# A seven-product scheme for the second channel product of an attention and MLP-mixer kernel

## The chip, the cores and the metric

One core of one Trainium2 chip runs the whole kernel in one launch. The core has five engines that run side by side and meet only at semaphores: TensorE (in the profile PE for its matmuls and PEld for its weight loads), VectorE (DVE), ScalarE (ACT), GpSimd (POOL) and SyncE (SP). The metric is the device time of one execution in microseconds (us); lower is better. Before the change it was 307.08 us, the median of three runs (306.64 to 309.66).

## The reference, cut to what matters

The input is attention over 4 batches, 8 heads, 768 tokens and 64 features per head, with a block mask, followed by a mixer MLP on 512 channels:

```python
scores = scale * np.matmul(q, k.transpose(0, 1, 3, 2))
...
attn_out = np.matmul(attn, v)                     # (4, 8, 768, 64)
x = attn_out.transpose(0, 2, 1, 3).reshape(4, 768, 512)
tok = np.einsum('ts,bsd->btd', w_tok, alpha1 * x + beta1)
u = x + lam * tok
a2 = alpha2 * u + beta2
ch = np.maximum(a2 @ w_ch1, 0.0) @ w_ch2          # 512 -> 2048 -> 512
return u + lam * ch
```

The last product, relu(...) @ w_ch2, is the "second channel product". Per batch it is a 768 x 2048 matrix times a 2048 x 512 matrix. The change concerns this product alone, and what makes room for it.

## The kernel before, in words

All steps of the program are short functions, registered under a letter by `@on`, and the text `ORDER` (L47 to L118) names them one after the other in the order in which they are emitted. `pin_order` (L121) keeps every engine in exactly that order, so the place of a word in the table is the place of its instructions in its engine's queue. `bank_order` (L138) keeps the eight PSUM banks apart: who writes a bank waits for all who read it last, whatever part of the bank they read. The table was written out by a planner and holds the bank numbers (`q8:1`) and the engine of some steps (`g14:a` for ScalarE, `g15:d` for VectorE).

The work of one batch, step by step:

- `q` (L575) makes 1024 scores per partition in two PSUM banks, `e` (L599) takes their exponential on ScalarE into an `eT` tile (eleven buffers, `NET`), `m` (L606) masks that tile in place on VectorE by a minimum with a 0 or 65504 mask (for head pairs 5 to 15; earlier pairs have the mask in the product), and `p` and `r` (L638, L642) multiply it with the values. `nt` and `n` (L646, L659) divide by the row sums and put the result into `x_sb`, which has room for three batches.
- `a`, `b`, `k`, `x` (L697 to L728) are the token mixing; `x` adds the product into `x_sb` in place, so that `x_sb` then holds u. `u` casts u to bf16 and `U` transposes it, by DMA on SP's queue or on TensorE, into `uT` (three buffers).
- `f` (L779) is the first channel product: for a half batch of 384 tokens and one of 16 blocks of hidden features, four matmuls of 384 columns. `g` (L791) adds the bias, takes the relu and writes bf16 into `hts`, on ScalarE or VectorE. `hts` has two buffers, each a half batch: [128 features, 16 blocks, 384 tokens].
- `h` (L813) is the second channel product. For each half batch `kk` and each of three groups of 128 tokens, 16 matmuls of 512 columns run through the 16 blocks (four steps `h` of four matmuls); the lam factor was put into the weights `w2b` beforehand by `S`. The last group is cut in two halves of 256 columns.
- `o` (L825) adds the finished bank to `x_sb` on VectorE, into a separate tile `ot`, and `s` (L835) sends that tile to HBM from SP's queue.

So `hts` of one half batch can be refilled while `h` works on the other half. Most of the table mixes the attention of a later head pair (`q e m p`) with the mixing of an earlier batch; from the end of the attention on, only `f`, `g`, `h`, `o` and `s` are left.

Of the kernel before, what the change touches and what calls it, by code (L numbers as in the profile page):

```python
# [36 lines left out]
TH = 256  # L37
NU = 9
NPE = 5
NET = 11  # L40
# [7 lines left out]
lv0 lk1 lq1 cq0 hm0 lt1 q0:2 q1:0 e0 q3:3 H1:2 q2:2 e1 hq1:d hk1:d lq2 e2 z480:3 z480:3 z480:3 q4:0  # L48
q6:1 q5:2 lk2 lv1 e3 cv0:d lq3 cq1:d e4 lt0 ck1:d p0:6 p1 p2 p3 e5 r4:7 q7:0 p4 e6 e7 lt2 lk3 n0
H2:5 H3:4 r5 hk2:d hq2:d lc2 lc0 q8:1 e8 r6 W2:6 hq3:d w2:d F21 cq2:d lc1 ck2:d q9:0 W3:5 q12:1 r7  # L50
e9 r8 e12 q11:0 n1 hk3:d H4:6 e11 cv1:d cq3:d q10:1 lk4 lv2 H5:7 q16:0 e10 p9:4 hq4:d q15:1 hk5:d
p10 e16 e15 p11 lq6 lq4 q13:0 hk4:d e13 hq5:d w3:d p12 W1:7 w1:d q14:1 W0:5 w0:d q25:0 p13 q19:3 e14
W4:5 r13:3 W5:2 n2 e25 ck3:d w4:d e19 lv4 lk5 lx3 q22:0 H6:4 e22 w5:d r14 q20:3 r15 H7:2 q17:0 hq6:d
r16 hk6:d q18:2 e20 L1 e17 L0 a0 e18 q24:3 q23:0 r17 b0 e24 hq7:d F22 cv2:d n3 k1:4 q26:3 k0:5 x1
cq4:d lv3 lc5 lk6 hk7:d e23 q21:0 p18:4 q28:1 e26 lx1 e21 e28 x0 q29:3 r22:5 p19 r23 q31:0 r24 r25
cq6:d r26 a1 F23 ck4:d lv6 ck5:d u1:d u0:d lw0 lq7 lw3 lc4 lw1 e29 b1 cv4:d n5 q30:1 p20 p21 H9:7
e31 p22 H8:6 q27:0 e30 n4 hq9:d cv3:d hk9:d U0:5 lw2 e27 q34:1 k3:4 hk8:a v0:d e34 lx2 p27:7 q33:0
lq5 x3 e33 hq8:d F24 p28 q32:2 a2 k2:6 q35:1 e32 p29 b2 u3:d q37:0 ck6:d F25 x2 q44:2 u2:d p30 r31:6
p31 e35 lk7 e44 r32 r33 U1:3 lx0 lv7 q39:2 r34 lq8 n6 F26 ah6 r35 k5:7 n7 M0 v1:a q40:1 ah7 e39 x5
e37 bh7 e40 bh6 F27 k4:6 q38:2 e38 L2 cv6:d q36:0 k7:2 B0 x4 F28 e36 cq7:a u4:d x7 u5:d q41:2 k6:6  # L60
lk8 lv8 x6 e41 p36:7 u7:a q43:0 U2:2 q42:2 u6:d v2:a U3:6 e43 p37 S6 v3:d p38 p39 p40 f15:6 f12:3
f10:2 e42 f14:0 g14:a g15:d f13:5 f29:6 f7:4 f8:1 S7 g12:d S4 g13:a g7:a S2 g10:d n8 S5 ck7:a g29:d
f6:2 f30:3 f23:5 f11:7 f28:6 cq5:d lv5 f9:0 g23:d g6:a g8:d f22:2 g11:d g9:d g30:d g28:a lq9 g22:d
f31:4 f0:5 f2:1 f25:7 f4:0 S0 g31:a f3:6 tq5 g2:d g3:d S1 g4:a g0:a N0 tk5 tk6 f27:2 f24:3 f5:0
f21:6 f26:1 f16:5 F29 g5:d g21:d O0 g24:d g26:d F30 S3 r40:4 g27:a g25:a cv5:a r41 tq7 g16:a r42 r43
r44 q47:0 n9 q51:3 q48:1 f17:5 lk9 e47 a4 f20:4 e51 e48 f1:0 f18:1 f19:2 g1:a b4 g20:d F31 k9:4
g17:a g19:a g18:d F32 q52:0 q53:3 q50:1 tq6 cq8:a k8:5 lv9 cv7:d m51 m48 x9 P7:d e52 p48:1 p51:4 m52
lq10 e53 cq9:a e50 x8 m53 p52 h0:0 F33 ck9:d p53 h1 lk10 lv10 nt17 ck8:d q49:3 q45:1 q46:2 tk8 tk7
h2 lq11 tq8 e49 F34 m50 e45 m49 h3 p49 p50 q59:1 q56:3 e46 o0 m47 m46 e59 u8:d tq9 tk9 e56 m59 u9:d
m45 m56 nt16 q58:2 h8:0 h9 P0:a e58 h4:2 h5 h10 F35 P4:d m58 h11 cq11:d P6:d o2 p45:3 lk11 p46 s0  # L70
ck10:a p47 cv8:d nt15 F36 h6 lv11 a5 q57:2 q62:3 q61:0 b5 e57 h7 e61 k11:4 e62 m57 lq12 p57:5 q60:0
o1 ck11:d P1:d x11 m62 q55:1 F37 e60 s1 q70:3 p58 p59 lk12 nt19 m61 F38 m60 h20:4 cq12:d e55 h21 m55
# [118 lines left out]
def kernel(  # L191
# [99 lines left out]
    b1_bc = wk.tile([P, DM], FP, name="b1_bc", tag="ot", bufs=4)  # L291
    a2T = pp.tile([P, 4], FP, name="a2T", tag="a2T")
    b1_bcb = pp.tile([P, DM], BF, name="b1_bcb", tag="b1_bcb")
    warm = pp.tile([P, 512], BF, name="warm", tag="warm")
    nc.vector.memset(warm[:], 0.0)

    def zero(w, i):
# [587 lines left out]
```

## Time and profile before

| what | value |
|---|---|
| median of three runs | 307.08 us (306.64 to 309.66) |
| the profiled execution, first to last instruction (its span) | 306.8 us; the page gives no other time of its own |
| mean granted TensorE clock | 1.000 |
| busy: TensorE matmuls / VectorE / ScalarE / GpSimd | 298.7 / 219.0 / 198.5 / 51.4 us |
| first matmul of the first `q` | 7.6 us into the span |
| last matmul ends, last `o` ends, span ends | 303.3, 303.8, 306.8 us |

Busy time counts an instant once when several instructions of an engine overlap; a row's mean duration counts each of them in full. The two differ on VectorE, ScalarE and TensorE, where the next instruction starts before the last one has ended, so an engine's cost per instruction is read from how far apart the starts lie in a stretch without waits, and its latency from the mean. A line such as `L820 PE MATMUL` belongs to a line of the kernel; the letters of the steps do not appear in the profile and are found by these lines.

### The profile page before, as it was taken

The page shows a single profiled execution, that of the slowest core. Times are in us where ns is not written, and L with a number is a line of the kernel's source. Part 1 is how long each engine was busy: PE and PEld are TensorE (multiplying, and loading weights), DVE is VectorE, ACT ScalarE, POOL GpSimd, SP SyncE. Part 2 cuts the span into 40 slices and gives each one's busy share as a digit, 9 for nine tenths or more (in the row PEclk, how much of TensorE's full clock was granted, in tenths as well). Part 3 has the DMA queues.
Part 4 walks back from the last instruction along what each step waited for, and adds up shares of the span by engine and source line. Part 5 has one row for each costly group of instructions (what it writes and reads, how often), then busy time and mean ns, then how long its engine had stood idle before and what let it go on. Part 6 is the DMA issues. An engine that isn't in the chain of part 4 may idle for free.

```text
span 306.8 us, 7748 instructions
## 1 busy us (share of the span) xinstructions
PE 298.7 (97%) x3276; PEld 195.2 (64%) x3301; DVE 219.0 (71%) x476; ACT 198.5 (65%) x262; POOL 51.4 (17%) x94
## 2 busy tenths in 40 slices
PE   8999999999999999999999999999999999999995
PEld 4577788766756676557666675556666585565443
DVE  3479999897979998865878697568778897412112
ACT  3799999745985996876954885276974961256000
POOL 5553655121334402310010000000000000000000
PEclk9999999999999999999999999999999999999999
DMA  6999999999999889941012345420002303100112
GB/s 144 177 238 186 133 195 198 203 193 178 118 146 178 133 158 150 153 63 30 2 28 60 87 88 88 112 60 2 2 2 61 96 2 84 39 2 0 67 68 106
DMA packets 48319, 30.92 MB, mean 101 GB/s; under 512 B 29004, under 2 KB 44124, under 8 KB 48284
## 3 DMA queue, kind: packets, MB, share of 16 engines
q0 software_dynamic: 15936, 15.21, 32.6%
q1 hardware_dynamic: 32132, 14.97, 22.9%
q8 instruction: 26, 0.43, 0.6%
q10 hardware_dynamic: 216, 0.24, 0.2%
q14 instruction: 9, 0.07, 0.1%
HBM read 31.19 MB, written 6.88 MB: 124 GB/s over the span
## 4 chain that ended last, share of the span: by engine, by line
PE 84%; DVE 10%; issue 2%; ACT 2%; DMA 1%; SPq 0%; DVEq 0%; ACTq 0%
PE psum L786 27%; PE psum L820 22%; PE psum L719 10%; PE psum L617 9%; PE psum L593 7%; PE psum L583 6%; DVE eT L611 3%; ACT eT L604 2%; DVE a1p L689 2%; DVE x_sb L652 1%; DMA sampi<-in_sampled_blocks_dram 1%; DVE a1p L695 1%; DVE ot L830 1%; PE psum L335 1%; PE psum L298 1%
## 5 line engine op out<-in xcount | busy, mean ns | idle before, releaser
L604 ACT ACTIVATE eT<-psum 128x1024 f16<-128x1024 f32 (+1 forms) x145 | 138.3, 1023 | 36.4 <-PE psum L593 31.8
L820 PE MATMUL psum<-w2b,hts 128*128 128x512 bf16 (+1 forms) x375 | 85.2, 370 | 2.1 <-issue 0.8
L786 PE MATMUL psum<-uT,w1b 128*128 128x384 bf16 (+1 forms) x512 | 85.4, 326 | 0.0
L611 DVE TENSOR_TENSOR eT<-eT,maskT 128x1024 f16<-128x1024 f16 x99 | 65.4, 686 | 8.3 <-ACT eT L604 8.0
L786 PEld LDWEIGHTS <-w1b 128*128 128x128 bf16 x512 | 49.2, 98 | 33.9 <-issue 1.1
L820 PEld LDWEIGHTS <-hts 128*128 128x128 bf16 x400 | 36.5, 98 | 37.6 <-issue 2.3
L800 ACT ACTIVATE hts<-psum,b1t 128x384 bf16<-128x384 f32 x73 | 38.8, 586 | 32.2 <-PE psum L786 31.6
L802 DVE TENSOR_SCALAR hts<-psum,b1t 128x384 bf16<-128x384 f32 x55 | 33.0, 615 | 28.3 <-PE psum L786 27.6
L617 PEld LDWEIGHTS <-eT 128*128 128x128 f16 x1152 | 42.6, 97 | 8.6 <-issue 1.3
L617 PE MATMUL psum<-vext,eT 128*128 128x65 f16 x1152 | 45.9, 193 | 0.0
L719 PE MATMUL psum<-a1p,wtokT 128*128 128x128 bf16 x576 | 36.0, 219 | 1.1 <-DVE a1p L695 1.0
L719 PEld LDWEIGHTS <-wtokT 128*128 128x128 bf16 x576 | 33.2, 98 | 5.3 <-issue 2.7
L830 DVE TENSOR_TENSOR ot<-x_sb,psum 128x512 f32<-128x512 f32 (+1 forms) x25 | 16.6, 663 | 20.1 <-PE psum L820 20.1
L583 PE MATMUL psum<-qx,kx 88*128 88x512 bf16 (+1 forms) x120 | 27.7, 348 | 0.2
L593 PE MATMUL psum<-qx,kx 64*128 64x256 bf16 x396 | 27.7, 271 | 0.0
L593 PEld LDWEIGHTS <-kx 64*128 64x128 bf16 x396 | 16.5, 94 | 10.1 <-issue 3.7
L728 DVE TENSOR_TENSOR x_sb<-x_sb,psum 128x384 f32<-128x384 f32 x32 | 17.4, 549 | 4.8 <-PE psum L719 4.6
L401 POOL DMA_DIRECT2D k<-in_k_dram x15 | 10.8, 717 | 35.8 <-ACT vext L383 17.4
L401 POOL DMA_DIRECT2D v<-in_v_dram x16 | 11.6, 724 | 25.1 <-ACT b1t L383 7.0
L689 DVE TENSOR_TENSOR a1p<-x_sb,a_bc 128x768 bf16<-128x768 f32 (+1 forms) x17 | 15.4, 908 | 0.3
L652 DVE TENSOR_TENSOR x_sb<-psum,rcp 128x256 f32<-128x256 f32 x33 | 14.0, 424 | 1.1
L583 PEld LDWEIGHTS <-kx 88*128 88x128 bf16 x120 | 10.2, 103 | 6.1 <-issue 1.8
(70 smaller groups left out, 160.8 us busy)
## 6 DMA issues: line engine op xcount, KB each, us to landing
out_dram<-ot SPq DMA_DIRECT2D x23, 256.0 KB, 2.1
v<-in_v_dram POOLq DMA_DIRECT2D x16, 192.0 KB, 4.7
k<-in_k_dram POOLq DMA_DIRECT2D x15, 192.0 KB, 5.0
q<-in_q_dram POOLq DMA_DIRECT2D x15, 192.0 KB, 6.2
w2b<-in_moe_w_ch_dram POOLq DMA_DIRECT2D x4, 512.0 KB, 11.1
w1b<-in_moe_w_ch_dram POOLq DMA_DIRECT2D x4, 512.0 KB, 12.0
wtk<-in_moe_w_tok_dram POOLq DMA_DIRECT2D x3, 384.0 KB, 7.5
mask_rows<-maskT SPq DMA_DIRECT2D x1, 576.0 KB
```

What stands on the lines that cost most here:

```text
L401: nc.gpsimd.dma_start(t[:], pair_ap(src, *batch(p)))
L583: nc.tensor.matmul(t[:, f : f + w], kx[h][0:KC, ts(jt, P)], qx[h][0:KC, c : c + w], start=True, stop=True,)
L593: nc.tensor.matmul(t[:, (2 * a + j) * TH : (2 * a + j + 1) * TH], kx[h][r, ts(2 * g + j, P)], qx[h][r, ts(th, TH)], start=True, stop=True,)
L604: nc.scalar.activation(eTs[n][:, c], t[:, c], AF.Exp, bias=EXPB, scale=SCALE)
L611: nc.vector.tensor_tensor(out=e, in0=e, in1=mask, op=ALU.min)
L617: nc.tensor.matmul(ops[key][:, t * VW : t * VW + D + 1], eTs[n][:, c : c + P], vext[n // NU % NV][:, a, jt, 0 : D + 1], start=(first and z ...
L689: nc.vector.tensor_tensor(out=a1p[p][:, :, c : c + w], in0=x_of(p, 0, NT, c, w), in1=per_col(a1_bc, p, NT, c, w), op=ALU.mult)
L719: nc.tensor.matmul(t[:, j, :], wtokT[:, s, ts(3 * g + j, P)], a1p[p][:, s, :], start=(s == 0), stop=(s == NT - 1),)
L786: nc.tensor.matmul(hps[i][:, 0:w], w1b[:, dk, ts(f, P)], uT[b][:, dk, hf * HS : hf * HS + w], start=(dk == 0), stop=(dk == 3),)
L800: nc.scalar.activation(hts[kk][:, f, :], t[:, 0:HS], AF.Relu, bias=b1t[:, f : f + 1], scale=1.0)
L802: nc.vector.tensor_scalar(out=hts[kk][:, f, :], in0=t[:, 0:HS], scalar1=b1t[:, f : f + 1], scalar2=0.0, op0=ALU.add, op1=ALU.max,)
L820: nc.tensor.matmul(cps[i][:, 0:w], hts[kk][:, nk, ts(m, P)], w2s[0][:, nk, lo : lo + w], start=(nk == 0), stop=(nk == 15),)
```

## The change

The half batches y = 0 and y = 1, the two halves h = 0 and 1 of the hidden blocks, and the two halves of the weights' rows and columns are taken as 2 x 2 block matrices, once for each of the three token groups q of 128 (named q in the code, not to be mixed up with the step `q`). Write A11, A12 (y = 0), A21, A22 (y = 1) for the quadrants of `hts`, each [128, 8 blocks, 128 tokens], and B11 to B22 for those of `w2b`, each [128, 8 blocks, 256 columns]. The seven products z of Winograd's form of Strassen's scheme, eight matmuls of 256 columns each, are

- z0 = A11 B11, z1 = S1 T1, z2 = S2 T2, z3 = S3 T3, z4 = A22 T4, z5 = S4 B22, z6 = A12 B21, with S1 = A21 + A22, S3 = A11 - A21, S2 = S1 - A11, S4 = A12 - S2 and T1 = B12 - B11, T2 = B22 - T1, T3 = B22 - B12, T4 = B21 - T2.

One PSUM bank serves a batch and a token group: z0, z2, z3 and z4 accumulate in its left half one after the other, and after each of them the half is read out; z1 and z5 accumulate in its right half; z6 begins the left half anew. The new steps are

- `T` (four in all): the sums of weight quadrants, VectorE, 2048 elements per partition each.
- `A` (four for each of 12 batch and token groups, 48 in all): the sums S1 to S4, VectorE, 1024 elements each; S3 and S2 are written over A21 and A11 in place, S1 and S4 go to tiles `ss` with three buffers.
- `h`: 84 steps of eight matmuls of 256 columns, in place of 100 steps of four.
- `o`: five additions per group straight into `x_sb`, three of 256 columns and two of 512, and one more at the very end (61), in place of 25 into `ot`.
- `s` sends rows of `x_sb` itself; 25 transfers as before.

Beside these, `m` leaves out four columns at each edge of every 128 tokens (`EDGE`), whose queries lie in the first and the last block and see everything: 960 elements instead of 1024. `eT` has ten buffers instead of eleven, `uT` two instead of three, `ot` and `warm` no longer have room of their own. The order table is new from end to end; in it, 88 of the 128 `g` (73 before) and 22 of the 32 `u` (16) are on ScalarE, and 12 of the casts of loaded heads (13).

```diff
-NET = 11
+NET = 10
...
-    lam_bc = wk.tile([P, DM], FP, name="lam_bc", tag="ot", bufs=4)
-    b1_bc = wk.tile([P, DM], FP, name="b1_bc", tag="ot", bufs=4)
+    lb = wk.tile([P, 2, DM], FP, name="lb", tag="tt", bufs=3)
+    lam_bc, b1_bc = lb[:, 0, :], lb[:, 1, :]
...
-        e = eTs[n][:].rearrange("p (a c) -> p a c", a=4)
+        c = slice(EDGE, P - EDGE)
+        e = eTs[n][:].rearrange("p (a t c) -> p a t c", a=4, t=2)[:, :, :, c]
         th, g = divmod(n % NU, 3)
-        mask = maskT[:, g, ts(th, TH)].unsqueeze(1).broadcast_to([P, 4, TH])
+        mask = maskT[:, g, ts(th, TH)].rearrange("p (t c) -> p t c", t=2)[:, :, c]
+        mask = mask.unsqueeze(1).broadcast_to([P, 4, 2, P - 2 * EDGE])
         nc.vector.tensor_tensor(out=e, in0=e, in1=mask, op=ALU.min)
...
-            uT[b] = wk.tile([P, 4, S + 16], BF, name="uT", tag="uT", bufs=3)
+            uT[b] = wk.tile([P, 4, S + 16], BF, name="uT", tag="uT", bufs=2)
...
+    HF = FF // P // 2
+    HD = DM // 2
+    def quadrant(b, q, y, h):
+        return hts[2 * b + y][:, h * HF : (h + 1) * HF, ts(q, P)]
+    def weights(h, c):
+        return w2s[0][:, h * HF : (h + 1) * HF, c * HD : (c + 1) * HD]
+    def quad(n, k):
+        b, r = divmod(n, 3 * k)
+        return (b,) + divmod(r, k)
+    def total(op, out, in0, in1):
+        nc.vector.tensor_tensor(out=out, in0=in0, in1=in1, op=op)
...
+    @on("T")
+    def _(j):
+        if j != 1:
+            w2t[j] = wk.tile([P, HF, HD], BF, name="w2t", tag="tt", bufs=3)
+        if j == 0:
+            total(ALU.subtract, w2t[0][:], weights(1, 1), weights(0, 1))
+        elif j == 1:
+            total(ALU.subtract, weights(0, 1), weights(0, 1), weights(0, 0))
+        elif j == 2:
+            total(ALU.subtract, w2t[2][:], weights(1, 1), weights(0, 1))
+        else:
+            total(ALU.subtract, w2t[3][:], weights(1, 0), w2t[2][:])
+    def new_sum(key):
+        sums[key] = wk.tile([P, HF, P], BF, name="ss", tag="ss", bufs=3)
+        return sums[key][:]
...
+    @on("A")
+    def _(n):
+        b, q, j = quad(n, 4)
+        a11, a12, a21, a22 = (quadrant(b, q, y, h) for y in range(2) for h in range(2))
+        if j == 0:
+            total(ALU.add, new_sum((b, q, 1)), a21, a22)
+        elif j == 1:
+            total(ALU.subtract, a21, a11, a21)
+        elif j == 2:
+            total(ALU.subtract, a11, sums[b, q, 1][:], a11)
+        else:
+            total(ALU.subtract, new_sum((b, q, 4)), a12, a11)
...
     @on("h")
-    def _(i, bank_=None):
-        i, r = divmod(i, 4)
-        kk, m, lo, w = part(i)
-        if r == 0:
-            cps[i] = bank(bank_, [P, DM])
-        for nk in range(4 * r, 4 * r + 4):
+    def _(n, bank_=None):
+        b, q, z = quad(n, 7)
+        if z == 0:
+            cps[b, q] = bank(bank_, [P, DM])
+        lhs = sums[b, q, 1 if z == 1 else 4][:] if z in (1, 5) else quadrant(b, q, z in (3, 4), z in (4, 6))
+        rhs = (weights(0, 0), weights(0, 1), w2t.get(2), w2t.get(0), w2t.get(3), weights(1, 1), weights(1, 0))[z]
+        side = z in (1, 5)
+        for nk in range(HF):
             nc.tensor.matmul(
-                cps[i][:, 0:w], hts[kk][:, nk, ts(m, P)], w2s[0][:, nk, lo : lo + w],
-                start=(nk == 0), stop=(nk == 15),
+                cps[b, q][:, side * HD : (side + 1) * HD], lhs[:, nk, :], rhs[:, nk, :],
+                start=(z in (0, 6) and nk == 0), stop=(nk == HF - 1), skip_group_check=True,
             )
...
     @on("o")
-    def _(i):
-        kk, m, lo, w = part(i)
-        b, hf = half(kk)
-        ots[i] = wk.tile([P, DM], FP, name="ot", tag="ot", bufs=4)
-        nc.vector.tensor_tensor(
-            out=ots[i][:, 0:w], in0=x_sb[:, b % NXB * NT + 3 * hf + m, lo : lo + w],
-            in1=cps.pop(i)[:, 0:w], op=ALU.add,
-        )
+    def _(n):
+        b, q, r = quad(n, 6)
+        last = (b, q) == (B - 1, 2)
+        y, lo, hi, c = ((0, 0, 1, 0), (0, 1, 2, 0), (1, 1, 2, 0), (1, 0, 2, 0), (0, 0, 2, 0), (0, 0, 1, 0))[r]
+        if last and r == 4:
+            lo = c = 1
+        sl = x_sb[:, b % NXB * NT + 3 * (1 - y) + q, lo * HD : hi * HD]
+        total(ALU.add, sl, sl, cps[b, q][:, c * HD : (c + hi - lo) * HD])
...
         nc.sync.dma_start(
-            out[b].rearrange("(p o) d -> p o d", o=NT)[:, 3 * hf + m, lo : lo + w], ots.pop(i)[:, 0:w]
+            out[b].rearrange("(p o) d -> p o d", o=NT)[:, o, lo:hi], x_sb[:, b % NXB * NT + o, lo:hi]
         )
```

A number after `h` counts 21 to a batch and seven to a token group, one after `A` 12 and four, one after `o` 18 and six. The first words of the last stretch of the new table, where the attention has ended and the first channel product is ending too, and its last words, are

```
f108:6 h77:0 f111:1 h70:2 f110:3 g104:a A44 A40 A36 o66 A41 h63:7 h78 f109:4 A45 A46
h79 f107:5 g110:a g107:a g108:d o54 A42 o60 o67 g109:d h71 g111:a h80 A47 o68 A37 A38
...
h83 h75 o71 h68 h69 o58 s11 s8 s20 s13 s23 s6 s21 s12 s22 s14 s24 s15 s18 h76 o64 s19
```

## Prediction

> **What bounds the kernel now.** I read the busy shares first, then the stretches of 15 us, then the chain for the pace of each kind of work, then the rows of the groups.
>
> ```profile
> PE 298.7 (97%) x3276; PEld 195.2 (64%) x3301; DVE 219.0 (71%) x476; ACT 198.5 (65%) x262; POOL 51.4 (17%) x94
> ```
>
> TensorE is the bound. Its matmul rows overlap, so 97% says little; the stretches show what stands beside it:
>
> ```profile
> 30.00:45.00 15.00, 14.67 (x234) 11.93 (x232) 14.64 (x36) 14.06 (x16) 9.29 (x15) 1.00 1.04 163
> 90.00:105.00 15.00, 14.83 (x180) 9.19 (x181) 14.43 (x37) 11.62 (x14) 6.20 (x11) 1.00 0.93 153
> 270.00:285.00 15.00, 14.95 (x90) 8.62 (x89) 3.09 (x5) 8.00 (x17) 0.00 (x0) 1.00 0.00 1
> 285.00:300.00 15.00, 14.95 (x74) 7.24 (x74) 3.16 (x5) 0.00 (x0) 0.00 (x0) 1.00 0.19 71
> ```
>
> The columns behind the length are PE, PEld, DVE, ACT, POOL, then clock, DMA share and GB/s. Twice VectorE is already as full as TensorE (14.64 and 14.43 of 15 us), and only behind the attention is it idle. The clock is 1.00 throughout. Paces come from the chain (start, length, what, how many):
>
> ```profile
> 57.02 17.64 PE psum L786 x108
> 177.47 1.29 DVE eT L611 x2
> 179.36 3.01 DVE eT L611 x5
> 187.18 2.17 PE psum L719 x36
> 282.77 0.86 PE psum L820 x4
> ```
>
> An `f` matmul takes 163 ns, a 512-column `h` matmul 216 ns, a 128-column one 60 ns, weight load included. A mask starts every 0.60 us although its row says 0.69. The tail's 256-column matmuls fill this stretch, where weight loads of 98 ns were busy 0.90 us, 9.2 loads, so 109 ns each:
>
> ```profile
> 301.00:302.00 1.00, 1.00 (x12) 0.90 (x10) 1.00 0.66 254
> ```
>
> ```profile
> L820 PE MATMUL psum<-w2b,hts 128*128 128x512 bf16 x343 | 82.1, 379 | 2.1 <-issue 0.8 <-DVE x_sb L652 0.3
> L611 DVE TENSOR_TENSOR eT<-eT,maskT 128x1024 f16<-128x1024 f16 x99 | 65.4, 686 | 8.3 <-ACT eT L604 8.0
> L800 ACT ACTIVATE hts<-psum,b1t 128x384 bf16<-128x384 f32 x73 | 38.8, 586 | 32.2 <-PE psum L786 31.6
> L802 DVE TENSOR_SCALAR hts<-psum,b1t 128x384 bf16<-128x384 f32 x55 | 33.0, 615 | 28.3 <-PE psum L786 27.6
> L830 DVE TENSOR_TENSOR ot<-x_sb,psum 128x512 f32<-128x512 f32 x23 | 15.7, 684 | 18.6 <-PE psum L820 18.6
> L695 DVE TENSOR_TENSOR a1p<-a1p,b_bcb 128x768 bf16<-128x768 bf16 x15 | 8.3, 555 | 0.4
> L477 DVE TENSOR_TENSOR w2b<-w2b,lam_bcb 128x1024 bf16<-128x1024 bf16 x8 | 5.4, 683 | 0.0
> L830 DVE TENSOR_TENSOR ot<-x_sb,psum 128x256 f32<-128x256 f32 x2 | 0.8, 420 | 1.5 <-PE psum L820 1.5
> ```
>
> Two prices per VectorE instruction follow: the mean (latency), and the mean less 0.085 us (0.686 against 0.60) when the next one doesn't depend on it.
>
> How full TensorE really is: every step of the old table at its pace (`f` 0.652, late `q` 0.254, early `q` 0.435, `p` 0.245, `k` 1.065, `h` 0.864 us) comes to 290.8 us. The first `q` starts at 7.6 and the last matmul ends at 303.3, so stalls cost only 4.9 us; 3.5 us follow it. Any gain must come from less matmul work, and stays only if VectorE and ScalarE keep up.
>
> **TensorE's part.** Removed: 92 full `h` steps of 0.864 and 8 half ones of 0.436, 83.0 us. Added: 84 steps of eight matmuls at 109 ns, 0.87 us each, 73.1 us. Saved: 9.9 us, all on the bounding engine. The ends for the pace are 108 ns (half of 216) and 125 ns (32 of them in 4.0 us busy, starts and waits included), with which nothing would be saved; I take 109, from the stretch without gaps. The weight loads, 672 instead of 400, hide: 98 ns fit in 109, and loads follow each other at 60 ns in L719.
>
> **VectorE's part**, at the price between independent starts. Added: 48 `A` of 1024 bf16 elements, the form of L477 (0.683, so 0.60): 28.8 us. Four `T` of 2048: L695 and L477 give 0.5 ns per element, so 1.195, less 0.085, 1.11 each: 4.4 us. `o`: per group three of 0.335 and two of 0.60, 2.2 us, 26.8 in all with the extra one, against 15.0. Taken off: 15 `g` to ScalarE, 8.3 us; 6 `u`, 2.8; 64 elements of each of 99 masks at 0.5 ns, 3.3. Casts: 0.3 more. Sum: 31 us more, 207.0 to 237.9 by this price (219.0 measured before: dependent ones cost more). Ends: `A` as slow as fp32 additions (L830, 1.04 ns per element) would be 25 us more; L477 and L695, with runs as short, speak against it. For the shorter runs of the mask I take the gain; without it 3.3 us return.
>
> **ScalarE's part.** 15 `g` and 6 `u` more, one cast less: 200.7 to 211.7 us.
>
> **The other queues.** GpSimd issues the same loads, the transposes on SP are the same. Freed by `s` being in place: `ot`. New waits: `nt` of batch 3 (`nt36`) needs slots that batch 0's output has left; its last `s` (`s4`) stands about ten TensorE us earlier, and such a transfer lands in 2.1 us: nothing. On SP, `s20` waits for `o70`, some eight `h` (7 us) before the end, with ten transfers of 256 KB queued behind it, five of them ready long ago, and one of 128 KB. 2.9 MB in all at the 377 GB/s that the last 7 us reach when busy (113 at a share of 0.30) are 7.6 us. The last `o` is 0.26 us longer (0.684 for 0.42) and its transfer 0.4 us (2.1 for 1.7). I take 0.7 us; the queue makes 0.7 to 3.
>
> **New waits of TensorE.** A bank is read between z0, z2, z3, z4 and z6: four hops of `o` per group, 3 x 0.42 + 0.68, 1.9 us, 23 us in all were nothing beside them; a gain is excluded, since the old `h` waited in mid-bank for nothing. The table always has another group's `h` (0.87 us each) or attention in between. In the tail 21 `h` and four `f` (20.9 us) face 12 `A` and 16 `o` (about 14 us) with three banks in turn: I take nothing. `hts` has no free buffer now: `g63`, the first into batch 1, must wait for all of batch 0's z3 and z4. The table puts attention there; that is in the next sum. Two buffers of `uT` and ten of `eT` I cost at nothing: `f` of batch 0 is over long before `U8`, and a score and its use stand 12.3 us of TensorE work apart at the median (7.2 before).
>
> **Where VectorE and ScalarE come up short.** I added the prices in the order of both tables; these are us of PE / DVE / ACT in the new one: to `r44` 49.4 / 40.3 / 47.0; to `h6` 61.0 / 60.8 / 63.1; to `h22` 48.6 / 43.6 / 45.5; to `h42` 57.5 / 46.7 / 39.5; to `p143` 12.8 / 13.0 / 4.9; to the end 51.5 / 33.5 / 11.6. In the second stretch all three are full. Cutting both tables in windows of 12, 15, 18, 21 and 24 us of TensorE work (six offsets each) and adding, per window, what the fullest engine has beyond TensorE gives 10.3, 6.1, 5.1, 5.3, 4.7 us now against 2.8, 1.4, 0.5, 0.4, 0.4 before: 7.5, 4.7, 4.6, 4.9, 4.3 more, 5.2 in the mean. I take 5.2, on top of the 4.9 there already. Ends: zero, if buffers carry work across; and the full durations, in the rival below.
>
> **Sum**, against the profiled span: 306.8 - 9.9 + 0.7 + 5.2 = 302.8 us. The median of the runs stands 0.3 above the span: 303.1.
>
> **Rival 1: the cover holds.** No extra stalls: 306.8 - 9.9 + 0.7 + 0.3 = 297.9 us. For it: 30 to 45 us, where PE, DVE and ACT are at 14.67, 14.64 and 14.06 of 15, and to 57.0 us the work (48.3 us) is only 1.1 us late. Against it: that was one stretch, not 61 us with ScalarE 2 us over.
>
> **Rival 2: VectorE becomes the bound (slower).** If sums and additions depend on each other so closely that each costs its full mean, the windows of 12 us, the distance between a score and its use, hold 23.2 us of excess against 8.6: 14.6 more. 306.8 - 9.9 + 0.7 + 14.6 + 0.3 = 312.5 us. Place: between `r44` and `h6`, where full durations give VectorE 69.7 us to TensorE's 61.0, and around `h42`, where seven `A` stand together. It decides from 9.2 us of extra stalls, and is 1% slower from 12.3. For it: 219.0 measured lies 40% of the way from 207.0 to the 237.5 that full means give. Against it: the masks at 0.60 above. The Trainium skill, VectorE: DVE Perf Modes, section "The DRAIN you can't avoid", says that the next instruction doesn't start until the pipe is empty. By that rule this rival would be the forecast; the trace, with starts 0.60 us apart for rows of 0.69, disagrees for independent instructions.
>
> **Rival 3: the gain is eaten.** With VectorE 40% of the way to the full means, the mean extra of the five windows (5.2 and, at full means, 12.0) becomes 7.9: 305.8 us, within 1%. For it, the same 40%; against it, the table can put independent work between dependent ones.
>
> **How the numbers follow.** About 1%, from 304.0 to 310.2 us, is what a measurement of this kernel can tell from no change. Forecast 0.48 (300.5 to 305, two thirds of it below 304.0), rival 1 0.16, rival 3 0.13, rival 2 0.23 (all but 0.01 beyond 310.2). Faster: 0.33 + 0.16 = 0.49; same 0.15 + 0.13 + 0.01 = 0.29; slower 0.22. The range, 298 to 311, leaves out half of rival 1 and about half of rival 2.
>
> **What would show it.** Right: 256-column `h` matmuls 109 ns apart; `A` rows near 0.68 us, masks near 0.65; VectorE busy near 250 us; TensorE waiting longest between about 57 and 125 us, for ScalarE or VectorE. The tail from the first of the last 21 `h` is some 21 us plus 4. Wrong: `A` at 1.2 us; matmuls waiting on `o` in the tail; TensorE waiting on `A` throughout; the last transfer landing over 3 us after its `o`; a granted clock below 1.00 after such waits.

## The result, and the profile after

The changed kernel takes 319.59 us (median of four runs, 318.20 to 320.94) against 306.86 us (306.06 to 309.66) for the kernel before on the same chip: a ratio of 1.041, interval 1.035 to 1.047. It is slower, by some 12.7 us, where 303.1 us were predicted, and it lies outside the range of 298 to 311 us. The profiled execution took 318.20 us with a span of 316.4 us, 9.6 us longer than the span of before. It is the shortest of the four; the other three have spans of 317.6 to 319.1 us and left no profile, so the account below is of 9.6 us and not of 12.7. All ratios in this document leave out executions more than 1.5% above the fastest of their kernel.

The page of the kernel after: busy times, then the TensorE, clock and DMA rows of the 40 slices (7.9 us each).

```profile
PE 292.7 (93%) x3573; PEld 220.1 (70%) x3573; DVE 247.8 (78%) x539; ACT 208.3 (66%) x287; POOL 50.3 (16%) x94
...
PE   7999997039999999999999999999999999999993
...
PEclk9999999558999999999999999999999999999999
DMA  6999999994772153799638134320000104400036
```

TensorE is busy 6 us less and VectorE 29 us more (9.9 and 31 were worked out). The loss is a hole: two slices, from 55 to 71 us, in which TensorE stands almost still, the clock granted to it falls to a half, and the DMA row reads 9. After the hole TensorE is full to the end. The stretches say the same (PE, PEld, DVE, ACT, POOL, then clock, DMA share, GB/s):

```profile
30.00:45.00 15.00, 15.00 (x257) 12.51 (x255) 14.16 (x35) 13.93 (x17) 9.52 (x16) 1.00 1.19 178
...
45.00:60.00 15.00, 8.17 (x130) 6.65 (x127) 8.80 (x28) 8.88 (x10) 4.46 (x10) 0.88 1.24 185
60.00:75.00 15.00, 6.20 (x75) 5.14 (x76) 2.40 (x8) 2.56 (x4) 0.71 (x1) 0.55 1.14 193
75.00:90.00 15.00, 14.88 (x121) 8.11 (x119) 14.55 (x33) 14.22 (x29) 3.20 (x8) 1.00 0.53 67
90.00:105.00 15.00, 15.00 (x216) 10.42 (x213) 14.05 (x31) 14.57 (x22) 2.12 (x4) 1.00 0.44 59
```

The kernel before has TensorE busy 15.00 of 15 us in both of the stretches with the hole:

```profile
45.00:60.00 15.00, 15.00 (x228) 12.03 (x225) 12.99 (x35) 12.81 (x17) 5.19 (x10) 1.00 1.15 201
60.00:75.00 15.00, 15.00 (x107) 9.21 (x106) 12.50 (x30) 7.78 (x18) 2.62 (x6) 1.00 1.21 179
```

In the kernel after, all four engines are idle for most of the time from 60 to 75 us while the DMA queues are at work: they wait for transfers. (The DMA share alone does not tell the two kernels apart: it is above 1 in both.) TensorE's waits (us in total, times, longest) name the one it is, and the chain of waits shows it whole (start, length, what):

```profile
PE psum L596 <- DMA kx<-rel: 15.5, 1, 15.5
```

```profile
53.36 0.71 SPq L555
...
54.16 14.51 DMA kx<-rel
...
68.80 0.61 PE psum L596 x4
```

L596 is the late `q`, L555 the transposing load `tk`. It is the score `q61`, the first of head pair 6 and the first in the new table to need a DMA transpose. SP's queue shows how late that transpose was, after and then before:

```profile
43.83 10.23 SPq L555 DMA_TRANSPOSE qx<-rel  x1
54.16 4.63 SPq L555 DMA_TRANSPOSE kx<-rel  x1
59.89 0.36 SPq L507 DMA_DIRECT2D maskT<-mask_rows  x1
```

```profile
66.34 5.93 SPq L552 DMA_TRANSPOSE kx<-rel  x2
73.48 0.36 SPq L504 DMA_DIRECT2D maskT<-mask_rows  x1
73.95 3.97 SPq L552 DMA_TRANSPOSE qx<-rel  x2
```

To issue one transpose took 10.23 and 4.63 us in the kernel after, 1.3 to 3 in the one before (two stand together in some rows), and the one of `kx` stood behind the one of `qx`. From issue to landing `kx` took 14.5 us against 5.6 to 7.9, in the views of the tile `kx` after and before:

```profile
DMA to landing us min/median/max: 14.5/14.5/14.5
```

```profile
DMA to landing us min/median/max: 5.6/6.7/7.9
```

The new table starts them at 44 and 54 us, into the loads of both channel weights (`w1b` landed 14.3 us and `w2b` 15.6 us after issue at the median; before, 12.0 and 11.1), and wants the first one at 53.4 us; the old table put 27 `f` in front and asked at 74.7 us. VectorE's queue was held by the same traffic: the cast `cq5` waited 9.6 us for its load.

Adding every step of the new table at its pace gives 49.7 us of TensorE work up to the first `f` and 231.2 us from there on. So the span divides into the following; the two rows of stalls are remainders, what is left of a stretch when the work at its pace is taken off.

| us | before | after |
|---|---|---|
| up to the first `q` | 7.6 | 7.1 |
| TensorE work | 290.8 | 280.9 |
| stalls up to the first `f` (57.0 us / 73.45 us) | 1.1 | 16.6 |
| stalls behind it | 3.8 | 6.4 |
| from the last matmul to the end | 3.5 | 5.3 |

By this account the saving of 9.9 us is there (the eighth product below bears it out). The front lost 15.5 us more than before, the rest of the table 2.6, the tail 1.8.

### The profile page after: what moved, and what is told of

It reads as the page before. It is cut to its first block, busy times and chain, and to the rows that moved or that the text cites. A ratio compares the mean times of both kernels' runs of the same rounds, so it can differ in the third digit from the quotient of the medians.

```text
span 316.4 us, 8394 instructions
## 1 busy us (share of the span) xinstructions
PE 292.7 (93%) x3573; PEld 220.1 (70%) x3573; DVE 247.8 (78%) x539; ACT 208.3 (66%) x287; POOL 50.3 (16%) x94
## 4 chain that ended last, share of the span: by engine, by line
PE 83%; ACT 7%; DMA 5%; DVE 2%; issue 1%; SPq 0%
PE psum L792 24%; PE psum L871 23%; PE psum L623 11%; PE psum L725 10%; PE psum L596 8%; ACT eT L607 5%; DMA kx<-rel 5%; PE psum L586 4%; ACT hts L806 2%; PE psum L301 1%; PE psum L338 1%; PE psum L770 1%; PE psum L463 1%; DVE a1p L695 0%; ACT vext L386 0%
## 5 line engine op out<-in xcount | busy, mean ns | idle before, releaser
L806 ACT ACTIVATE hts<-psum,b1t 128x384 bf16<-128x384 f32 x88 | 48.7, 584 | 37.6 <-PE psum L792 27.8
L617 DVE TENSOR_TENSOR eT<-eT,maskT 128x960 f16<-128x960 f16 x99 | 61.9, 651 | 2.2 <-ACT eT L607 1.7
L596 PE MATMUL psum<-qx,kx 64*128 64x256 bf16 x396 | 30.5, 273 | 15.7 <-DMA kx<-rel 15.5
L830 DVE TENSOR_TENSOR x_sb<-x_sb,psum 128x256 f32<-128x256 f32 (+1 forms) x61 | 31.2, 516 | 12.0 <-PE psum L871 11.8
L871 PE MATMUL psum<-w2t,hts 128*128 128x256 bf16 x288 | 35.3, 273 | 0.0
L596 PEld LDWEIGHTS <-kx 64*128 64x128 bf16 x396 | 15.6, 94 | 26.5 <-issue 19.1
L808 DVE TENSOR_SCALAR hts<-psum,b1t 128x384 bf16<-128x384 f32 x40 | 24.2, 614 | 11.8 <-PE psum L792 11.2
L871 PE MATMUL psum<-w2b,hts 128*128 128x256 bf16 x192 | 24.6, 273 | 0.0
L871 PE MATMUL psum<-w2b,ss 128*128 128x256 bf16 x192 | 24.6, 273 | 0.0
L871 PEld LDWEIGHTS <-ss 128*128 128x128 bf16 x192 | 18.2, 98 | 2.5 <-issue 0.4
L386 ACT CAST ub<-x_sb 128x384 bf16<-128x384 f32 x22 | 11.2, 514 | 10.3 <-DVE x_sb L734 10.2
L830 DVE TENSOR_TENSOR ss<-hts 128x1024 bf16<-128x1024 bf16 x24 | 16.2, 683 | 0.9 <-ACT hts L806 0.8
## 6 DMA issues: line engine op xcount, KB each, us to landing
w2b<-in_moe_w_ch_dram POOLq DMA_DIRECT2D x4, 512.0 KB, 15.6
w1b<-in_moe_w_ch_dram POOLq DMA_DIRECT2D x4, 512.0 KB, 14.3
```

The source lines that it names most:

```text
L596: nc.tensor.matmul(t[:, (2 * a + j) * TH : (2 * a + j + 1) * TH], kx[h][r, ts(2 * g + j, P)], qx[h][r, ts(th, TH)], start=True, stop=True,)
L617: nc.vector.tensor_tensor(out=e, in0=e, in1=mask, op=ALU.min)
L806: nc.scalar.activation(hts[kk][:, f, :], t[:, 0:HS], AF.Relu, bias=b1t[:, f : f + 1], scale=1.0)
L808: nc.vector.tensor_scalar(out=hts[kk][:, f, :], in0=t[:, 0:HS], scalar1=b1t[:, f : f + 1], scalar2=0.0, op0=ALU.add, op1=ALU.max,)
L830: nc.vector.tensor_tensor(out=out, in0=in0, in1=in1, op=op)
L871: nc.tensor.matmul(cps[b, q][:, side * HD : (side + 1) * HD], lhs[:, nk, :], rhs[:, nk, :], start=(z in (0, 6) and nk == 0), stop=(nk == H ...
```

## The experiments

The theory: TensorE takes its queue in order, and the front of the new table asks for DMA transposes some 20 us earlier than the old one, in the middle of a backlog on the DMA engines. The rivals: VectorE's sums are the bound (the prediction's rival 2), the clock makes the loss, or the transposes are slow by themselves. Times are medians; the ratio is to the kernel before, measured beside each run (306.7 to 308.1 us).

**The sums on VectorE.** All `A` and `T` return at once and the products take plain quadrants and weights.

```diff
     @on("A")
     def _(n):
+        return
...
     def _(j):
+        return
```

> Edit: the kernel after without its operand sums: the 48 steps A and the 4 steps T are left out, the products take plain quadrants and plain weights in their place (so the second channel product is wrong), the seven products and the additions o stay. Some 33 us of VectorE work are gone. Backlog theory: the wait at the first transposed score stays at 14 to 16 us and the time at 316 to 320 us, within 1% of the kernel after. VectorE-bound rival: the time falls by 8 us or more, to below 311 us.

318.23 us, ratio 1.039 (1.029 to 1.049); span 316.9. VectorE was busy 216.4 us instead of 247.8, and the time stayed within the spread of the two kernels' runs (317.29 to 321.55, and 318.20 to 320.94):

```profile
PE psum L596 <- DMA kx<-rel: 15.2, 1, 15.2
```

31 us of VectorE work are worth nothing that these runs can show: rival 2 is refuted as the cause. Nor did the part behind the hole get shorter: from the first `f` to the end it is 243.6 us here and 243.2 in the kernel after.

**An eighth product.** The third product of every group is done twice (the output is wrong by it).

```diff
-        for nk in range(HF):
+        for nk in [*range(HF), *range(HF if z == 2 else 0)]:
```

> Edit: the kernel after with an eighth product in every group (the third one is done twice, so the result is wrong): 12 x 8 matmuls of 256 columns more, 10.5 us of TensorE at the measured 109 ns. If TensorE bounds the part behind 75 us, as its windows say (15.00 of 15 us busy), the time rises by 8 to 11 us, to 327 to 331 us: the saving of the seven-product scheme was real and was only outweighed. If VectorE bounds it, the time rises by less than 4 us.

329.12 us, ratio 1.072 (1.067 to 1.078), 9.5 us above the kernel after by the medians, 11.5 by the spans (327.9). One product in every group costs about what its 96 matmuls at 109 ns make, 10.5 us. So the product left out was worth that much, and the loss lies elsewhere.

**The mask's traffic away.** The late pairs' mask (a table of 576 KB sent to HBM by `N0` and brought back by `O0`) is left out; a fill takes its place, so pairs 5 to 15 are not masked.

```diff
-        nc.sync.dma_start(maskT[:], mask_dr.rearrange("(p g) w -> p g w", p=P))
+        nc.gpsimd.memset(maskT[:], F16MAX)
-... lk8 lv8 N0 tq6 tk6 O0 e40 ...
+... lk8 lv8 tq6 tk6 O0 e40 ...
```

> The changed kernel without the mask's way through HBM: the write of 576 KB is left out and the read of 576 KB is replaced by a memset on GpSimd (so the late pairs are not masked). Theory (bandwidth of the DMA engines): 1.15 MB less at some 200 GB/s is 5 to 6 us less, the wait of 15.5 us at q61 falls to 8 to 11 and the time to 312 to 315 us. Rival (the order on SP's queue or the cast cq5 alone sets it): the wait stays over 13 us.

314.89 us, ratio 1.026 (1.020 to 1.032); span 312.0.

```profile
PE psum L596 <- DMA kx<-rel: 10.9, 1, 10.9
```

The wait is 4.6 us shorter, the first `f` starts 4.3 us earlier (68.96 for 73.25, both in the timeline, which has it 0.2 us ahead of the chain), and the span is 4.4 us shorter: what the front loses, the end loses. That it is the mask's bytes which cost this is not shown: with the traffic kept and only put behind the transposes (below) the wait is 10.5. In both runs `kx` was issued at 46.0 us instead of 54.2, and landed 18 us later.

**The weights' traffic away, filled by GpSimd**, in the kernel after and, as a control, in the kernel before; neither loads the channel weights.

```diff
-        nc.gpsimd.dma_start(w1b[:, g, :], moe_w_ch1[ts(g, P), :])
+        nc.gpsimd.memset(w1b[:, g, :], 0.02)
...
+        nc.gpsimd.memset(w2s[0][:, 4 * g : 4 * g + 4, :], 0.02)
```

> The changed kernel with the loads of both channel weights (eight of 512 KB) left out: GpSimd fills the tiles with a constant instead, so the output is of other weights; everything else is the same. Theory (the backlog of loads on the DMA engines holds the transposes of pair 6 and q5): some 4 MB at 200 GB/s, 20 us of DMA time, go from the stretch to 60 us; the wait at q61 is under 4 us, the clock 0.99 or more, the time 297 to 304 us, which is then also the price of the seven-product scheme by itself. Rival 1 (a DMA transpose takes 14 us whatever runs beside it): the wait stays over 10 us, 314 or more. Rival 2 (VectorE and ScalarE are the bound): no such wait, yet over 308 us.

> The control: the kernel before with the same loads left out. Theory: its loads are hidden behind the first channel product, so it changes by less than 1%: 304 to 308 us. If the loads cost the kernel before too, it falls as far as the changed one.

After: 317.41 us, ratio 1.033 (1.027 to 1.038). Before: 318.76, ratio 1.041 (1.033 to 1.049). In the changed kernel the wait for `kx` was down to 0.4 us and one for `qx` of 3.1 us was left, with 3.49 and 1.79 us to issue the transposes in place of 10.23 and 4.63; `kx` landed 6.3 us after its issue in place of 14.5, `qx` 9.1 in place of 20.4. (The wait itself compares badly: TensorE came to `q61` at 66.9 us and not at 53.4.) But both kernels met a new hole of 8.3 us, made by the fills themselves. VectorE in the changed kernel, with its queue of GpSimd behind it:

```profile
39.89 7.47 DVE L388 COPY vext<-v 128x768 f16<-128x768 f16 x1
49.13 1.52 DVE L388 COPY vext<-v 128x768 f16<-128x768 f16 x1
```

```profile
39.33 1.82 POOL L446 MEMSET w1b<- 128x2048 bf16 x1
41.84 3.56 POOL L446 MEMSET w1b<- 128x2048 bf16 x2
45.32 1.82 POOL L452 MEMSET w2b<- 128x2048 bf16 x1
```

A copy that takes 0.35 us elsewhere stood until four fills were over. The pair of runs shows that the transposes are quicker without the weights' traffic; its times say nothing of what that is worth.

**Half of it away, filled by VectorE.** `w1b` alone is not loaded, and VectorE fills it.

```diff
-        nc.gpsimd.dma_start(w1b[:, g, :], moe_w_ch1[ts(g, P), :])
+        if g > 1:
+            nc.vector.memset(w1b[:, g, :], 0.02)
...
+    nc.vector.memset(w1b[:, 0:2, :], 0.02)
     first_cast(0)
```

> Edit: the kernel after without the four loads of the first channel weights (w1b is filled with a constant by VectorE, half of it in VectorE's idle time at the start); the kernel leaves out these weights, so its output is not the reference's. The second weights are loaded as they were. Backlog theory: half of the weight traffic is gone from 30 to 60 us, nothing is filled by GpSimd this time, the 15.5-us wait at the first transposed score falls below 9 us and the time to 307 to 314 us. If the transposes are slow of themselves (their descriptors or SP's issuing), the wait stays at 14 to 16 us and the time above 317 us.

315.04 us (311.6 to 317.6). The ratio, 1.019 (1.010 to 1.027), is of the two runs at 311.6 and 313.5, which are within what I expected; the profile is of the longest, with a span of 315.9 us. Its waits (the late `q` is L598 here), its two transposes and the view of `kx`:

```profile
PE psum L598 <- DMA qx<-rel: 2.6, 1, 2.6
PE psum L625 <- DVE kx L389: 2.2, 1, 2.2
```

```profile
52.80 4.13 SPq L557 DMA_TRANSPOSE qx<-rel  x1
57.02 1.32 SPq L557 DMA_TRANSPOSE kx<-rel  x1
```

```profile
DMA to landing us min/median/max: 5.6/5.6/5.6
```

`kx` was issued 2.9 us later than in the kernel after and landed some 6 us sooner, 5.6 us after its issue in place of 14.5, so the rival of transposes that are slow by themselves falls. The wait for `kx` went from 15.5 to 0.4 us, but 9 us of that only mean that TensorE came to `q61` at 62.4 us and not at 53.4: the fills (3.47 us at the start, two of 1.76 later) delayed VectorE, and TensorE waited behind it at 42 and 46 us (1.6 and 2.2 us). The first `f` started 8 us earlier (65.20 for 73.25), and this execution lost nearly all of it again, with 2.6 us for `qx`, 2.1 us for `uT` at 139 us and further spells at half clock.

**A busy wait.** 62 matmuls of 512 columns on the warm-up tile stand ahead of `q61`, so that TensorE works through the hole on nothing.

```diff
-... tq5 U2:0 q61:1 U1:6 ...
+... tq5 U2:0 z512:2 z512:2 (62 in all) z512:2 q61:1 U1:6 ...
```

> The changed kernel with 62 more matmuls of zeros, 512 columns each, right ahead of q61 (13.4 us of TensorE that stand in the wait and give nothing). The wait itself stays. If the throttled clock behind the wait (0.55 in that stretch) costs time, the clock reads 1.00 and the span is 1.5 to 3 us shorter, about 314 to 316; if it costs nothing, the time stays within 1 us of the changed kernel.

315.74 us, ratio 1.028 (1.024 to 1.033); span 314.0, clock 0.998 instead of 0.972. From the start of `q61` to the first `f` it takes 2.5 us instead of 4.5, and the span is 2.4 us shorter: that is what the half clock behind the wait cost. The Trainium skill, TensorE: Matmul & The Clock Gate, in the table of the two states, has the throttled state return after an idle window of about 3.4 us. Here the clock was 0.63 on the mean from 55 to 60 us and 0.50 from 60 on, so it fell at about 56.3 us, some 3 us into a wait that began at 53.4, which is close to that.

**The last rows early.** Every `s` of the last batch stands right behind its `o`.

```diff
-... h69 o58 s11 s8 s20 s13 s23 s6 s21 s12 s22 s14 s24 s15 s18 h76 o64 s19
+... o52 s11 s8 s6 s15 s12 s13 s14 ... o69 s23 ... o70 s20 ... o57 s21 ... o71 s24 ... o58 s18 h76 o64 s19
```

> The changed kernel with only the s steps moved: seven output transfers of batches 1 and 2 that are ready long before go out ahead of the last ones, so that in the last 7 us only those of batch 3 are left. Theory: the span now ends 4.6 us after the last o, against 3.0 before; with the queue empty it is 3.0 to 3.5, so 1 to 1.6 us less, 318 us or a little below. If the queue in the tail costs nothing, the time is the changed kernel's.

317.56 us, ratio 1.033 (1.030 to 1.037). The span ends 3.35 us after the last `o` instead of 4.6: the queue of transfers behind `s20` cost 1.3 us. (The span itself is 317.7 us, since this execution was 3.1 us later at its first transposing load, 40.60 for 37.54, long before the edit; its wait for `kx` is 15.0.)

**The front repaired by order alone**, all work kept. The mask's way out put behind the transposes of pair 6:

```diff
-... N0 tq6 tk6 O0 ...
+... tq6 tk6 N0 O0 ...
```

> The changed kernel, but the write of the mask rows (N0, 576 KB on SP's queue) stands behind the transposes of pair 6 instead of ahead of them. If that write is what holds the transposes on their queue, the wait at q61 falls from 15.5 us to under 10 and the time to 314 or less. If the loads of the weights and heads that fill the DMA engines hold them, the wait stays between 13 and 18 us and the time between 316 and 322.

318.35 us, 1.037 (1.032 to 1.042): the wait fell to 10.5 us, which is neither of the two outcomes that I had named, `qx` came 3.0 us late in its place, span 315.9. `q61` alone put back behind U1, U3, `r` and three `f`:

```diff
-... U2:0 q61:1 U1:6 ... f13:7 n8 a4 g5:d ...
+... U2:0 U1:6 ... f13:7 n8 a4 q61:1 g5:d ...
```

> The changed kernel, but q61, the first score step that needs a DMA transpose, stands behind U1, U3, the last values of pair 4 and f3, f5, f13 (some 5 us of TensorE work that does not need it). Theory (one in-order wait): TensorE waits 15.5 us at q61 for the transposes of pair 6, and everything behind q61 in its queue waits with it; 5 us of work moved ahead of it takes about 5 us off, 312 to 315 us. Rival (VectorE and ScalarE are the bound, the wait only shows where they fall behind): no change beyond 1 us, 317 to 320.

322.31 us, 1.050 (1.043 to 1.057). TensorE now waited 6.1 us for `v`, which stood behind `cq5` on VectorE (10.4 us for its load), 3.0 for `w1b`, 2.5 for `uT` and 3.1 for `qx`. With 15 `f` ahead of all late scores (the expectations count one `f` too many here and with the 26 below), and `cq5` later:

```diff
-... cq5:d F33 F27 ... tq5 U2:0 q61:1 U1:6 ... g13:a q58:0 q49:1 q47:2 e58 e47 f6:7 f14:6 ...
+... F33 F27 ... U2:0 U1:6 ... g13:a f6:7 f14:6 ... ck7:d cq5:d tq5 ... f17:0 g15:d g1:a g4:a g17:a
+q61:1 e61 q58:0 q49:1 q47:2 e58 e47 ...
```

> The changed kernel, but q61 and the other early scores of pairs 5 and 6 stand behind the first 16 f of batch 0, as do the cast cq5 and the transpose tq5 that wait for a late load. Theory (one in-order wait): some 15 us of TensorE work stands ahead of q61, so nearly the whole 15.5 us and the throttled clock behind it go: 300 to 305 us, with the clock at 0.99 or more. Rival (VectorE and ScalarE are the bound): the waits come back in the stretch to 125 us as waits for sums and evictions, 312 us or more.

321.66 us, 1.049 (1.045 to 1.053): 7.3 us of waits for `g`, itself behind the weights' products `S`, which waited 7.8 us for `w2b`. The same, with `S` later and SP's order as before (tq5 N0 tk5 tq6 tk6 O0 behind `cq5`):

> The changed kernel with the order of its first 80 us as in the kernel before: the first 16 f of batch 0 come ahead of the late scores, the transposes of pairs 5 and 6 stand behind that of q5 on SP, and the scaling of the last weights (S0, S1, S3) and the cast cq5 stand behind the first evictions. Theory (the DMA engines, full until about 70 us, deliver later than the new table asks; moving the wait of one engine uncovers the next): no wait of TensorE over 3 us is left between 45 and 90 us and the time is 300 to 306 us. Rival (VectorE and ScalarE are the bound): the stalls reappear before 125 us, 312 us or more.

316.33 us, 1.030 (1.024 to 1.037), the best of these: 5.1 us for `kx` and 5.3 in several waits for ScalarE are left. From there, 11 more `f` in one block ahead (26 in all) and the last rows early:

```diff
-... g17:a q49:1 q47:2 ...
+... g17:a f27:1 g27:d f22:4 f28:2 g22:a f20:3 g28:a f19:1 ... f2:2 g21:a g2:a q49:1 q47:2 ...
```

> Edit: the front of the kernel before, fuller than in the run with 16 first-layer steps ahead (316.33 us): 27 of batch 0's f stand ahead of the first score that waits for a DMA transpose, and the last rows leave early as in the run that cut 1.3 us from the tail. Backlog theory: in the kernel before the first transposed score came after 27 f, at 74.7 us, and waited for nothing; with the same 27 ahead the remaining waits of the 16-f run (5.1 us of TensorE on kx, 9.2 of VectorE on the mask) have 7 more us of cover and fall below 2 us each; the time is 303 to 309 us, at or just below or above the kernel before. If VectorE or the order table behind 75 us set the time, it stays above 313 us.

321.13 us, 1.045 (1.037 to 1.053): missed. `kx` is down to 1.7 us, but behind the block TensorE had little left but scores, which wait for exponentials, and it idled there:

```profile
70.00:75.00 5.00, 4.73 (x30) 2.64 (x27) 0.62 (x1) 3.88 (x10) 0.00 (x0) 1.00 1.43 167
75.00:80.00 5.00, 2.22 (x28) 1.04 (x28) 2.31 (x4) 4.51 (x6) 0.00 (x0) 1.00 0.61 171
80.00:85.00 5.00, 2.05 (x19) 1.55 (x19) 4.63 (x10) 4.38 (x5) 0.00 (x0) 0.52 0.00 0
85.00:90.00 5.00, 2.93 (x42) 2.07 (x40) 5.00 (x11) 1.94 (x2) 2.25 (x4) 0.80 0.45 65
```

From 80 to 90 us VectorE is busy 9.63 of 10 us (masks, the scaling of the second weights, their sums), with a DMA share of 0 in the first half: here it is VectorE and ScalarE that hold TensorE up, and no transfer, though VectorE had idled for 6.2 us up to 77.7 us, until the mask was back from HBM.

The same with these 11 `f`, and the six others of batch 0, set between the scores:

```diff
-... g17:a q49:1 q47:2 e49 e47 m49 q53:1 e53 ...
+... g17:a q49:1 f27:6 q47:2 e49 f22:7 e47 g27:d f28:6 q53:1 g22:d f20:7 e53 g28:d q48:2 f19:6 ...
```

> Edit: as the run with 16 first-layer steps ahead of the first score that needs a DMA transpose, and the other 16 f of batch 0 not in one block ahead of the scores (the run with 27 ahead) but one between each two scores and between the next chains; last rows out early. The 27-ahead run lost its time behind 75 us, where scores followed each other with only ScalarE's exponentials between them (TensorE 2.05 to 2.93 of 5 us busy). If the cause is transfers and chains without cover, the f's fill both gaps: TensorE's waits on kx and on ScalarE fall to 4 us or less together and the time to 305 to 312 us. If 16 f ahead are too few for the transposes whatever comes between, 3 to 5 us of wait on kx remain and the time is 312 to 317 us. If the clock and the later waits are set by the masks and the second weights on VectorE, it stays at 316 to 321 us.

324.18 us, 1.052 (1.042 to 1.063): missed too. 5.9 us for `kx`, and 7.5 for `g` on ScalarE and VectorE, which take `g`, exponentials and masks in the order that I gave them. The next ones moved the loads: head loads of pairs 7 and 8 held back until behind the weights; then head loads ahead of the second product's weights; then loads behind a flag that `cq5` precedes.

```diff
-... lw2 lx2 lq5 lk7 lx0 lv7 lq8 lk8 lv8 lv5 ...
+later:  ... lw2 lx2 lq5 lx0 lv5 lk7 lv7 lq8 lk8 lv8 ... (flags behind cq5)
+first:  ... lk6 lq5 ... lw2 lv5 lq7 lk7 lv7 lx3 lx1 lx2 lx0 ... lq8 lk8 lv8 ...
+gated:  ... lk6 lq5 ... lw2 lv5 ... lq7 lk7 lv7 lx3 lx1 lx2 lx0 lq8 lk8 lv8 tq5 (flag behind cq5)
```

> The changed kernel with the five head loads of pairs 7 and 8 (needed from about 90 us on) issued behind the last weights and the loads of pair 5, and held until q5 has landed; the casts that use them stand later. Theory (bandwidth): some 2 MB of reads leave the stretch from 44 to 60 us, so the transposes of pair 6 and q5 land 6 to 10 us earlier: wait at q61 below 9 us, 306 to 313 us. Rival (the order on SP's queue): the wait stays over 13 us and the time over 316.

> The changed kernel, order of TensorE and ScalarE untouched, but the loads in the order of need: the loads of pair 5 ahead of the channel weights, the second channel weights (2 MB, needed from about 95 us on) behind them, their scaling by lam on VectorE just ahead of the weight sums T, the cast of q7 behind that of q5; and the output transfers as in the run before. Theory (what is queued ahead of it on the full DMA engines sets when q5 and the transposes of pair 6 arrive): the wait at q61 falls from 15.5 us to under 6, the clock to 0.99 or more, the time to 298 to 306 us. Rival (VectorE and ScalarE are the bound): 312 us or more.

> The changed kernel with all its loads and the order of TensorE and ScalarE untouched, but the loads that are not needed before 75 us (heads of pairs 7 and 8, the second channel weights) held on GpSimd until q5 has been cast, q5 and v5 ahead of them, the mask's write behind the transposes of pair 6, the lam scaling ahead of T, and the output transfers early. Theory: with no backlog beside them the transposes of pair 6 land 5 to 9 us after their issue, the wait at q61 is under 6 us, 298 to 308 us. Rival 1 (a transpose takes 14 us whatever runs beside it): wait over 10 us, 314 or more.

Later: 328.97 us, 1.071 (1.062 to 1.081); `q5` itself then sat behind the weights, from 45.19 to 68.2 us, and the waits for `kx` were 22.5 us. First: 322.13, 1.048 (1.042 to 1.053); the weights, issued from 50 to 56 us, now met the transposes, wait 15.3. That order with `q61` behind the three `f` as well:

> The run before with q61 also behind U1, U3, the last values of pair 4 and f3, f5, f13. Theory: if some wait at q61 is left, these 5 us of work cover it and the time is 0 to 5 us lower; if the wait has gone, the time is the same within 1 us.

324.94 us, 1.058 (1.051 to 1.065), with 5.8 us of wait for `kx` and 4.1 for `qx`: no faster, against the expectation. Gated: 324.03, 1.055 (1.048 to 1.062). The transposes of pair 6 came sooner:

```profile
43.36 6.04 SPq L555 DMA_TRANSPOSE qx<-rel  x1
49.51 3.43 SPq L555 DMA_TRANSPOSE kx<-rel  x1
```

`kx` landed 6.4 us after its issue, and TensorE, which came to `q61` at 54.0 us as in the kernel after, waited 2.1 us there in place of 15.5. This is the plainest showing of the cause: no load is left out, the second weights and the heads of pairs 7 and 8 only come later (and the mask's way out stands behind the transposes, which was worth 5 us above). But the next transpose, issued at 60.35 us right behind the four loads of the second weights (57.5 to 60.5), met these: 9.6 us for `qx`, and another 3.7 for a later `kx`. The first `f` started 14 us earlier than in the kernel after (59.39), and the span was still 5.9 us longer.

What follows: the transposes are slow beside the weights' loads (from issue to landing `kx` took 14.5 us; 5.6 without `w1b`'s loads, 6.3 without both weights', 6.4 with the second weights' held back), and a move in the order hands the wait to the next transfer or the next engine. That an order exists which keeps the saving is neither shown nor excluded; none of the ten orders of the front that I tried beat the kernel before, and nearly all came out above the time that the theory had promised, several of them where the rival of VectorE and ScalarE had put them (312 us or more). Most of the waits were for transfers all the same, but not all, and no re-ordered kernel was run without the sums; so how much of the rest of the loss these two engines make in them is open.

## Why the prediction was wrong

**The step that failed** is "The other queues. GpSimd issues the same loads, the transposes on SP are the same", costed at nothing. The same transfers were issued, but the new table took the first late score from 74.7 to 53.4 us, and the prediction did not ask what a transpose costs there. Where the old table has them, behind 27 `f`, they take 1.3 to 3 us to issue and 5.6 to 7.9 to land. At these prices the new order would have cost next to nothing too: `kx` could be issued at 46.0 us (as it was with the mask's way out behind it) and would have landed by 53.9. What came was 10.23 and 4.63 us to issue, 14.5 to land and a wait of 15.5 us, and the front lost 15.5 us more than before. The half clock behind the wait, which I named as a sign of being wrong and priced nowhere, is 2.4 us of the span.

The trace of before had a warning, in the rows of other transfers in that stretch. The loads of `q` (192 KB) took this long from 20 to 80 us, where 6.2 us is their median over the whole run:

```profile
DMA to landing us min/median/max: 8.1/9.3/14.7
```

An estimate with these 14.7 us: `kx`, issued at 46.0 us, would land at 60.7 and make 7 us of wait, half of what came. The DMA share, 1.04 from 30 to 45 us, was no such warning: it was 1.41 from 65 to 70 us, where the old table's transposes landed in 5.6 to 7.9 us.

The same gap is in "a score and its use stand 12.3 us of TensorE work apart": that looks behind a score, and the wait was in front of it. The sign "TensorE waiting longest between about 57 and 125 us, for ScalarE or VectorE" did not come: the longest wait began at 53.4 us and was for a transfer. And in "where VectorE and ScalarE come up short" the first stretch, up to `r44`, read 49.4 / 40.3 / 47.0, no shortage at all; the hole lies just there, since a sum of work sees no transfer.

**Right, by its own steps.** TensorE's part: the 256-column matmuls run 109 ns apart (16 in 1.75 us, 8 in 0.87), and the eighth product shows the price (9.5 to 11.5 us for 10.5); that 280.9 us of work remained is taken over into the account above and fits it. VectorE: busy 247.8 us ("near 250"); the rows in the profile after:

```profile
L617 DVE TENSOR_TENSOR eT<-eT,maskT 128x960 f16<-128x960 f16 x99 | 61.9, 651 | 2.2 <-ACT eT L607 1.7 <-ACT b1t L386 0.2
L830 DVE TENSOR_TENSOR ss<-hts 128x1024 bf16<-128x1024 bf16 x24 | 16.2, 683 | 0.9 <-ACT hts L806 0.8
L830 DVE TENSOR_TENSOR x_sb<-x_sb,psum 128x256 f32<-128x256 f32 x38 | 15.6, 416 | 6.3 <-PE psum L871 6.2
L830 DVE TENSOR_TENSOR w2t<-w2b 128x2048 bf16<-128x2048 bf16 x2 | 2.4, 1221 | 0.0
```

The masks have the 0.65 us and the sums the 0.68 us named ahead; `o` waits for TensorE and not the other way round.

**Off in size, and the kind not shown.** "Where VectorE and ScalarE come up short" was taken as 5.2 us; behind the first `f`, where its stretches lie, the remainder grew by 2.6 us (6.4 for 3.8). That VectorE's sums are behind it is not borne out: without them that part of the span was no shorter (243.6 us for 243.2). ScalarE's share and the paces themselves were not tested. The tail's 0.7 us became 1.8 (5.3 for 3.5), within its 0.7 to 3, and 1.3 of it is the queue of transfers.

**The rivals.** By arithmetic, without the front's extra 15.5 us, the span would have been 300.9 us, between the forecast and rival 1; no run came near it. Rival 2 ended on the side where the time fell, but by another mechanism, and its own is refuted. No rival was about a transfer that is wanted earlier: that one was missing.

## What to carry to other kernels

When a table of work is made anew, list for every transfer the time at which its first user now stands, and price the transfer by what others cost in that stretch of the old trace: its own landing time in the old place (5.6 to 7.9 us here) says little of the new one (14.5). An in-order engine makes one late operand into a hole for all of its work. And a hole in a stretch full of loads was not repaired here by moving one step: the next transfer, or the next engine, took its place.

## What the runs showed of the hardware

- Beside the loads of the channel weights a DMA transpose took 10.23 us to issue and 14.5 to 20.4 us from issue to landing; without the weights' loads 1.79 to 3.49 us, and 6.3 (`kx`) and 9.1 (`qx`). So loads from GpSimd's queue delay transposes from SP's: the Trainium skill, DMA: Bandwidth & Descriptors, section "Rules for kernel authors", says that all issuing queues run on the same 16 DMA engines and interleave, and the trace agrees.
- A 768-element copy on VectorE (0.35 us alone) stood for 7.47 us beside GpSimd's fills of 1.8 us each, while a two-operand step and a copy out of PSUM beside them kept their 0.54 us. The Trainium skill, SBUF — State Buffer, section "SBUF: two separate sides", calls the port that the two engines share a lock held for one whole instruction; here the copy got through only after four fills.
- In the wait the granted clock fell to 0.50, and working on nothing through it gave 2.4 us back.
- The mean DMA share did not tell slow transfers from quick ones: transposes landed in 5.6 to 7.9 us at shares of 1.41 and 0.96 (before, from 65 to 75 us, in steps of 5), and in 14.5 us at 1.00, 1.25 and 1.20 (after, from 55 to 70 us).
